# One attention and feed-forward kernel: a 16-bit shift in the weight decoding, softmax sums from the products, dummy transposes, and a second p buffer

## The chip, the cores and the metric

The kernel runs on one core of a Trainium2 chip. A core has five engines that follow their own instruction queues in order: PE (TensorE, products and transposes), DVE (VectorE), ACT (ScalarE), POOL (GpSimd) and SP (SyncE), which here issues all transfers. The metric is the device time of the core in microseconds, the median of several runs; lower is better.

## The reference

For 4 batches of 768 positions and 8 heads of 64, each position attends to its 31 neighbours and to 24 block summaries (the maximum of 32 keys, the mean of 32 values). The result, as x of 512 columns, goes through a layer norm and a two-layer network in double-precision weights, and is added to itself.

```python
k_sum = k.reshape(B, H, nb, block, D).max(axis=3)
v_sum = v.reshape(B, H, nb, block, D).mean(axis=3)
mask_l = np.abs(pos[:, None] - pos[None, :]) < window
scores_s = scale * np.einsum('bhsd,bhnd->bhsn', q, k_sum) + np.log(block)
scores_all = np.concatenate([np.where(mask_l, scores_l, -1e9), scores_s], axis=-1)
a = np.exp(scores_all - np.max(scores_all, axis=-1, keepdims=True))
a = a / (np.sum(a, axis=-1, keepdims=True) + 1e-09)
x = np.matmul(a, np.concatenate([v, v_sum], axis=2))      # then (B, S, 512)
xn = (x - mu) / np.sqrt(var + 1e-06) * g_ln
out = x + np.maximum(xn @ w_ch1, 0.0) @ w_ch2             # 512x2048, 2048x512, float64
```

## The kernel before, in words

The 3072 positions are 24 tiles T of 128. Attention works in 48 blocks t = 2T + hh: four heads of one tile. The keys that a block needs (158 neighbours' positions and 24 summaries) lie side by side in one operand of 184 to 192 columns, so that scores, softmax and the product with v each take one pass. The feed-forward part works in pairs of tiles, g = 0 to 11, in steps s = 8g + j: `g1` makes 256 of the 2048 hidden columns (tile h), `g2` multiplies them back into x (tile a). Each operand is split into two float16 halves, and three products of the halves stand for one in full precision. Relu writes hh (ACT) and the rest hl (DVE), and PE needs both.

Batch 0 (blocks 0 to 11, steps named `early_...` and `...0`) is done in float32 from whole tensors loaded at the start, since no scale for float16 is known yet: `fetch_k0`, `fetch_q` (qw), `fetch_v0` (vw), `fetch_tail` (vst: 32 more rows of v, and 24 rows of block means that `batch_v0` makes with PE and copies with ACT). A block does `early_k` (kx), `early_qk` (s), `softmax` (DVE subtracts the mask, scales and takes the minimum in one custom instruction into p and mn; ACT takes the exponential and, with `accum_out`, the row sums), `early_transp` (PE turns p, ACT copies it: pp to pT), `early_pv` (o; then rc = 1 / (sum + 1e-9) on DVE, and x = o times rc on DVE for t < 4, on ACT behind that). From block 12 on, transposes of p and of xn go over DMA, operands are float16 halves, POOL makes the lower half of p (`transp`, tile p from p), and every block uses the one buffer `prob[0]`, tag "p"; batch 0 alternates between "p" and "p2".

Beside batch 0, the weights are loaded (`fetch_w`, raw: 32 pieces of 128 x 512 doubles), decoded from double to single precision by integer operations on DVE (`dec_w`), squared on ACT for a scale per block of pieces (`scale_w`), and split into float16 halves (`conv_w`, wp). A piece is a pair of 32-bit words per weight, low word first; the decoded word stands 3 bits to the left of the high word's place, with the low word's top 3 bits at its end.

The order of each engine's queue is written at build time. `Plan` records every operation, estimates costs (`cost`), simulates the engines (`schedule`, with a clock for PE that needs 3200 columns in each 3.41 us), and in `improve` keeps the best of 32 simulated orders. `Plan.issue` (L333 to L349) writes the operations in order of their planned starts; all instructions therefore carry line L349 in the profile, and groups are told apart by their tiles. On the chip each queue runs in that order and waits where a tile is not ready. Buffers are tags: `work(tag, ...)` reuses the space of the tag's earlier tile when that one is dead; HOMES lists the tags that a kind of tile takes in turn. PSUM has four pools (s, o, h, a) of two buffers.

Of the kernel before, what the change touches and what calls it, by code (L numbers as in the profile page):

```python
# [15 lines left out]
F16 = mybir.dt.float16  # L16
U32 = mybir.dt.uint32
# [13 lines left out]
NE = 192  # L31
NG = TT // 2
# [8 lines left out]
EH = 4  # L41
# [13 lines left out]
AWAY = 24  # L55
LOADS = [("fetch_k0", 0), ("fetch_k0", 1), ("fetch_q", 0), ("gain",), ("fetch_blocks",), ("fetch_k0", 2), ("fetch_k0", 3)]
# [3 lines left out]
    ksg=("qke", "k0_0", "k0_1"),  # L60
# [35 lines left out]
class Plan:  # L96
# [11 lines left out]
    def __init__(self):  # L108
        self.ops, self.slots, self.prev, self.uses = [], {}, {}, {}
        self.joined = False  # L110
# [87 lines left out]
    def cost(self, engine, op, a, k, ins, outs):  # L198

        free = lambda x: math.prod(n for _, n in x.ap[1:])  # L200
        n = max(free(x) for x in ins + outs) if engine != "tensor" else free(a[0])
        if engine == "sync":
            x = (outs + ins)[0]
            return self.ISSUE.get(self.names[self.stage][0], 380), x.ap[0][1] * free(x) * mybir.dt.size(x.dtype) / (200.0 if "transpose" in op else 360.0)
        if engine == "tensor":
            dt = ins[-1].dtype
            if dt == F32R:
                return 0.443 * max(n, 256) + 4.5, 0.0
            if dt == F16 or op == "transpose":
                return max((1 if dt == F16 else 2) * n / 2.4 + 3.0, 28.0), 0.0  # L210
            return max(2 * n / 2.4 + 2.0, 100.0) * 2 if ins[0].ap[0][1] > D else 2 * n / 2.4 + 53.0, 0.0
        psum = any(x.space == bass.MemoryType.PSUM for x in ins)
        pointers = sum(1 for x in ins[1:] if free(x) == 1)
        if engine == "scalar":
            extra = ("accum_out" in k) + sum(isinstance(k.get(x), bass.AP) for x in ("scale", "bias"))
            weights = self.names[self.stage][0] in ("dec_w", "conv_w")
            return n / 1.2 + (51 if psum else 93) + 93 * extra + 35 * weights, 0.0
        if engine == "vector":
            fixed = {"tensor_tensor_reduce": 78, "reciprocal": 90}.get(op, 70) + 61 * pointers
            fixed += 119 * (self.box(ins[0])[1] == D)  # L220
# [28 lines left out]

    def slack(self, x, y):  # L250

        name, a = self.names[x.stage]
        if x.engine == "tensor":
            if name in ("g1", "g2"):
                return SLACK2 * (a[0] >= 24)
            return SLACK * (name in ("qk", "pv", "batch_s"))
        late = name in ("load_q", "load_k", "load_v", "softmax", "transp", "pv") and a[0] >= LATE
        late |= name[:5] == "batch" and a[0] >= 2
        late |= name in ("ln", "lnT") and a[0] >= LATE // 2
        late |= name in ("g1", "g2") and a[0] >= 24  # L260
        if not late:
            return 0.0
        return SLACKD if y.engine == "sync" else SLACKE

    def schedule(self, rank, after, back):
# [11 lines left out]
        port, half = 0.0, 0  # L277
# [3 lines left out]
        for _ in range(count):  # L281
# [17 lines left out]
            if e == "tensor" and not back:  # L299
                while t >= tick + self.TICK:  # L300
# [14 lines left out]
            for j, wait in before[i]:  # L315
                ready[j] = max(ready[j], free[e] if wait is None else end[i] + wait)
                left[j] -= 1
                if not left[j]:
                    heapq.heappush(coming[self.ops[j].engine], (ready[j], j))
        return start, end  # L320

    def improve(self, rank, after, then, rounds):

        best = None
        for _ in range(rounds):
            rank = [r if x.first is None else -1e9 + x.first for r, x in zip(rank, self.ops)]
            start, end = self.schedule(rank, after, False)
            if best is None or max(end) < best[0]:
                best = max(end), start, end
# [3 lines left out]
    def issue(self, nc):  # L333
        for x in self.ops:
            x.first = in_front(self.names[x.stage], x.engine)
        after = [self.waits(x) for x in self.ops]
# [9 lines left out]
        self.time, self.start, self.end = best  # L346
        for _, i in sorted(zip(best[1], range(len(after)))):
# [6 lines left out]
def body(ctx: ExitStack, tc, qt, qa, qe, kt, ks, va, vb, vs, g_ln, w1, w2, blocks, out):  # L354
# [18 lines left out]
    vst = [cp.tile([P, 2, 4, D], F32, name=f"vst{i}") for i in range(NV)]  # L373
# [10 lines left out]
    tails = [x.rearrange("p h j d -> p h (j d)") for x in vst]  # L384
# [6 lines left out]
    vw = [work(f"vw{T}", f"vw{T}", [P, DM])[:] for T in range(NT)]  # L391
# [23 lines left out]
    def clear():  # L415
# [83 lines left out]
    def batch_v0(c):  # L499
        if c == 0:  # L500
            bt["ps", 0] = psum("a", "v0", [P, DM])
        x = vw[c] if c < NT else vend
# [3 lines left out]
        if c == NT:  # L506
            for r in (32, 96):
                v = r // D
                for i in range(NV):
                    nc.scalar.copy(  # L510
                        tails[i][r : r + NB, :, v * P : v * P + P],
                        bt["ps", 0][r : r + NB, :].rearrange("p (h x) -> p h x", h=2)[:, :, v * P : v * P + P],
# [118 lines left out]
    def softmax(t, pr):  # L631
        T = t // 2
        var = 0 if T % NT == 0 else (2 if T % NT == NT - 1 else 1)
        if pr == 0:
            st[t, "p"] = prob[t < NEARLY and t % 2]
            st[t, "mn"] = work("mn", f"mn{t}", [P, 4], F32, 2)
            st[t, "sum"] = work("sum", f"sum{t}", [P, 4], F32, 2)
        p, mn, sm, ps = st[t, "p"], st[t, "mn"], st[t, "sum"], st[t, "s", pr]
        late_ = t >= NEARLY

        heads = [(2 * pr + u, 2 * pr + u, bt["mask", T // NT][:, var]) for u in range(2)] if late_ else [
            (2 * v + pr, 2 * pr + v, emask[:, var] if v else msk[:, var]) for v in range(2)
        ]
        for u, (j, i, mk) in enumerate(heads):
            w = mk.shape[1]
            nc.vector.tensor_tensor_reduce(
                p[:, i, :w], ps[:, u, :w], mk, -1.0 if late_ else -QSCALE, 3.0e38, ALU.add, ALU.min,
                mn[:, j : j + 1],
            )
        scale = -1.0  # L650
        if late_:
            m2, (scale, plus) = mn[:, 2 * pr : 2 * pr + 2], bt["c", T // NT]
            nc.gpsimd.tensor_scalar(m2, m2, plus, 0.0, ALU.mult, ALU.add)
        for j, i, mk in heads:
            x = p[:, i, : mk.shape[1]]
# [22 lines left out]
    def fetch_tail(T):  # L678

        for v in range(2):  # L680
            nc.sync.dma_start(
                tails[T % NV][v * D : v * D + BLK, :, v * P : v * P + P],
# [45 lines left out]
    def early_pv(t, pr):  # L728
        T, hh = divmod(t, 2)
        near = vw[T].rearrange("p (h j d) -> p h j d", h=2, j=4)[:, hh]  # L730
        tail = tails[T % NV].rearrange("p h (v u d) -> p h v u d", v=2, u=2)[:, hh, :, pr]
        if pr == 0:
            st[t, "o"] = psum("o" if t < 8 else "s", f"o{t}", [P, 8, D])
        ps, e = st[t, "o"][:, :4], st[t, "pt", pr]
        spare_cols = st[t, "o"][:, 4:6].rearrange("p a b -> p (a b)")
        with pl.unit():
            for _ in range(t < WARMV):
                nc.tensor.transpose(spare_cols, ident[:], ident[:])
            both = ps.rearrange("p (v u) d -> p v u d", v=2)[:, :, pr]
            nc.tensor.matmul(both, e[:, 1, :], tail, start=True, stop=False)  # L740
            for v in range(2):
                j = 2 * v + pr
                nc.tensor.matmul(ps[:, j, :], e[:, 2 * v, :], near[:, j], start=False, stop=v == 1)
# [3 lines left out]
        nc.vector.tensor_scalar(rc[:], st[t, "sum"][:], 1e-9, None, ALU.add)  # L747
# [4 lines left out]
        if t < PVS:  # L752
            nc.vector.tensor_tensor(xo, ps, rc.unsqueeze(2).to_broadcast([P, 4, D]), ALU.mult)
        else:
            for j in range(4):
                nc.scalar.activation(xo[:, j], ps[:, j], AF.Copy, scale=rc[:, j : j + 1])
# [72 lines left out]
    def dec_w(m):  # L829
# [130 lines left out]

    def attend(t):
# [18 lines left out]
        if t % 2 and t < 8:  # L980
            norm(t // 2)

# [126 lines left out]
```

## Time and profile before

| | |
|---|---|
| median of 3 runs | 637.73 us (633.65 to 638.5) |
| the profiled execution, its own time | 638.03 us |
| its span, first to last instruction | 636.2 us |
| PE, DVE, ACT, POOL busy | 610.9, 450.8, 391.5, 207.8 us |
| mean granted TensorE clock | 0.984 |

A group's row gives engine, operation, output and input tiles, shapes, count, busy time and mean nanoseconds of one, then the idle time of the engine in front of the group and who ended it. In a timeline a row begins with its start and length in us; a bracket is the idle time before it and the instruction that ended it. In the view by stretches a row has, after the stretch and its length, the busy time of PE, PEld, DVE, ACT and POOL with their instruction counts, the granted clock, the DMA share and GB/s. PE's matmuls are pipelined, so that the length of one is longer than the step to the next; the same holds in part for DVE and ACT, where the cost of an instruction in a full queue is the step from its start to the next start.

### The profile page before, as it was taken

What the parts mean: (1) busy time and instruction counts of PE and PEld (TensorE: products, weight loads), DVE (VectorE), ACT (ScalarE), POOL (GpSimd) and SP (SyncE); (2) the same over time, 40 slices, a digit from 0 to 9 for tenths busy, and PEclk for the clock granted to TensorE, in tenths of its full rate; (3) what the DMA queues carried; (4) which work ended last, traced back from release to release, by engine and by line L of the source; (5) the groups of instructions that cost most, each with busy time, mean ns of one, the idle gap of its engine ahead of it and who ended that gap; (6) DMA issues with size and microseconds to landing.
All of it is one profiled execution on the core that took longest, in us unless ns stands there. A gap on an engine that the chain in (4) does not pass through costs nothing.

```text
span 636.2 us, 13437 instructions
## 1 busy us (share of the span) xinstructions
PE 610.9 (96%) x4611; PEld 433.3 (68%) x4611; DVE 450.8 (71%) x1190; ACT 391.5 (62%) x1036; POOL 207.8 (33%) x412
## 2 busy tenths in 40 slices
PE   8957899999999899999979999999999999999997
PEld 6746776765776676776757677677677666666665
DVE  3899889999779998878989797657447734422212
ACT  3998798888888868778877577645446531110100
POOL 4221312024455545555555354333223321100000
PEclk9988799999999999999998999999999999999999
DMA  8980487526986977798778657465335412110000
GB/s 281 349 297 22 133 280 237 183 74 165 269 194 175 216 185 187 152 254 211 192 189 177 121 141 170 116 125 125 84 93 116 102 37 60 25 51 1 18 16 34
DMA packets 124997, 93.15 MB, mean 146 GB/s; under 512 B 84864, under 2 KB 107392, under 8 KB 124928
## 3 DMA queue, kind: packets, MB, share of 16 engines
q1 hardware_dynamic: 124928, 92.29, 55.7%
q8 instruction: 36, 0.59, 0.4%
q14 instruction: 33, 0.27, 0.1%
HBM read 66.27 MB, written 6.29 MB: 114 GB/s over the span
## 4 chain that ended last, share of the span: by engine, by line
PE 52%; DVE 25%; DMA 8%; ACT 6%; POOL 4%; issue 4%; SPq 1%; DVEq 0%; ACTq 0%; POOLq 0%
PE a L349 23%; PE h L349 23%; DVE x L349 3%; DVE p L349 3%; DMA ksg<-in_kt 3%; DVE wf L349 2%; ACT p L349 2%; PE o L349 2%; DVE hl L349 2%; PE s L349 2%; POOL p L349 2%; DVE qhl L349 2%; DVE kl L349 2%; DVE v L349 2%; DVE wp L349 1%
## 5 line engine op out<-in xcount | busy, mean ns | idle before, releaser
L349 PE MATMUL h<-xs,wp 128*128 128x256 f16 x2304 | 278.2, 276 | 6.7 <-DVE hl L349 4.8
L349 PEld LDWEIGHTS <-wp 128*128 128x128 f16 x2304 | 226.7, 99 | 53.6 <-DVE hl L349 5.2
L349 PE MATMUL a<-wp,hh 128*128 128x512 f16 (+1 forms) x768 | 226.5, 377 | 0.3 <-DVE x L349 0.3
L349 PE MATMUL a<-wp,hl 128*128 128x512 f16 x384 | 144.7, 377 | 0.2 <-DVE hl L349 0.2
L349 ACT ACTIVATE hh<-h 128x512 f16<-128x512 f32 x96 | 56.6, 589 | 123.3 <-PE h L349 99.3
L349 DVE SCALAR_TENSOR_TENSOR hl<-h,hh 128x512 f16<-128x512 f32 x96 | 65.7, 685 | 86.8 <-ACT hh L349 86.6
L349 PEld LDWEIGHTS <-hh 128*128 128x128 f16 x784 | 75.3, 98 | 61.7 <-issue 0.9
L349 ACT ACTIVATE p<-p,mn,sv 128x184 f32<-128x184 f32 x144 | 76.0, 530 | 24.3 <-POOL mn L349 20.9
L349 POOL TENSOR_TENSOR p<-p,p 128x512 f16<-128x512 f32 x72 | 72.3, 1010 | 35.0 <-ACT p L349 33.2
L349 PEld LDWEIGHTS <-hl 128*128 128x128 f16 x392 | 38.3, 98 | 45.4 <-DVE hl L349 1.1
L349 DVE CUSTOM_DVE_ANT_0 p<-s,mask 128x184 f32<-128x184 f32 x144 | 42.2, 343 | 16.6 <-POOL p L349 10.0
L349 POOL TENSOR_SCALAR mn<-mn,sv 128x2 f32<-128x2 f32 x72 | 32.4, 451 | 58.3 <-DVE mn L349 57.3
L349 POOL TENSOR_TENSOR x<-x,rc 128x256 f32<-128x256 f32 x36 | 25.5, 709 | 75.5 <-DVE x L349 75.4
L349 DVE SCALAR_TENSOR_TENSOR x<-a,wsc,x 128x512 f32<-128x512 f32 (+1 forms) x48 | 35.5, 739 | 19.6 <-PE a L349 19.2
L349 ACT ACTIVATE kh<-ksg,sv 128x368 f16<-128x368 f32 x72 | 42.7, 595 | 10.0 <-POOL ksg L349 9.9
L349 DVE SCALAR_TENSOR_TENSOR kl<-ksg,sv,kh 128x368 f16<-128x368 f32 x72 | 44.5, 643 | 3.3 <-PE s L349 3.2
L349 DVE SCALAR_TENSOR_TENSOR v<-vst,sv,v 128x256 f16<-128x256 f32 x72 | 40.4, 588 | 2.3 <-ACT v L349 2.0
L349 POOL COPY ksg<-ksum 128x48 f32<-128x48 f32 x72 | 24.3, 338 | 47.9 <-DMA ksg<-in_kt 44.5
L349 DVE TENSOR_REDUCE x<-o 128x256 f32<-128x512 f32 x36 | 24.6, 685 | 16.2 <-PE o L349 15.9
L349 ACT CAST p<-p 128x512 f16<-128x512 f32 x72 | 33.1, 509 | 0.3
L349 ACT ACTIVATE v<-vst,sv 128x512 f16<-128x512 f32 x36 | 25.6, 716 | 8.8 <-PE o L349 7.2
L349 PEld LDWEIGHTS <-qhl 128*128 128x128 f16 x288 | 24.4, 99 | 5.2 <-issue 0.3
(124 smaller groups left out, 786.0 us busy)
## 6 DMA issues: line engine op xcount, KB each, us to landing
raw<-in_w SPq DMA_DIRECT2D x32, 512.0 KB
ksg<-in_kt SPq DMA_DIRECT2D x72, 184.0 KB
out_x<-x SPq DMA_DIRECT2D x23, 256.0 KB
qw<-in_qt SPq DMA_DIRECT2D x36, 128.0 KB
vst<-in_va SPq DMA_DIRECT2D x36, 128.0 KB
qs<-in_qt SPq DMA_DIRECT2D x36, 128.0 KB
vst<-in_vb SPq DMA_DIRECT2D x84, 32.0 KB
bst<-in_ks SPq DMA_DIRECT2D x12, 192.0 KB
```

What stands on the lines that cost most here:

```text
L349: getattr(getattr(nc, self.ops[i].engine), op)(*a, **k)
```

## The change

Decoding (`dec_w`): the low halves of the high words are overwritten in place with the low words' top 16 bits shifted right by 13, a tensor_scalar over 16-bit elements; one scalar_tensor_tensor then puts the sign, the top exponent bit and these three bits together with the shifted word. Before it was a tensor_scalar and two scalar_tensor_tensors.

Batch 0's softmax: the exponentials no longer write sums. vw and the vst tiles get a column of ones beside each pair of heads (130 columns for 128), so the products give the sums in o, and rc is made from them. The v loads become two transfers per tile; memsets write the ones. In the order of heads, mn and p now agree.

Dummy transposes: a step `spare`, recorded after block 3, is one transpose of the identity into pool "a". The simulation notes every pause of PE over 800 ns between its place and the first operation that needs its PSUM slot, and `issue` writes further copies of that transpose into these pauses, up to 800 ns before the next planned operation.

Late p: blocks from 12 on alternate between "p" and a new tile p3 in the tag "k0_0". The key buffers ksg go from ("qke", "k0_0", "k0_1") to ("qke", "k0_1", "qw4"), and the mask emask moves into "qke". EH = 6 puts the transposes of blocks 4 and 5 into pool "h" as well.

```diff
-EH = 4
+EH = 6
+NV2 = 2 * D + 2
+FILL_IN, FILL_END = 500, 800
-    ksg=("qke", "k0_0", "k0_1"),
+    ksg=("qke", "k0_1", "qw4"),
...
+    def watch(self):
+        spare = [i for i, x in enumerate(self.ops) if self.names[x.stage][0] == "spare"]
+        self.opens = spare[0] if spare else None
+        self.closes = {i for i, x in enumerate(self.ops) if self.opens in x.after}
...
+                if i == self.opens:
+                    opened = t
+                closed |= i in self.closes
+                at = max(free[e], opened or t)
+                while not closed and t - at > FILL_IN and t - at > FILL_END:
...
+                    fills.append(at)
+                    at += 112 if warm else 224
+                    columns += 256
...
-        for _, i in sorted(zip(best[1], range(len(after)))):
+        for _, i in sorted([*zip(best[1], range(len(after))), *((t, -1) for t in fills)]):
+            if i < 0:
+                op, a, k = self.ops[self.opens].calls[0]
+                getattr(nc.tensor, op)(*a, **k)
+                continue
...
-    emask = work("emask", "emask", [P, 3, NE])[:]
+    emask = work("qke", "emask", [P, 3, NE])[:]
...
+        for x in vw:
+            nc.vector.memset(x[:, :, :: NV2 - 1], 1.0)
...
-        for x in vst:
+        for x in tails:
             nc.gpsimd.memset(x[:], 0.0)
+            for v in range(2):
+                nc.gpsimd.memset(x[v * D : v * D + BLK + NB, :, v, :: NV2 - 1], 1.0)
...
     def go_late():
-        nc.gpsimd.memset(prob[0][:, :, NC:], 0.0)
+        late["p"] = prob[0], work("k0_0", "p3", [P, 4, NE])
+        for x in late["p"]:
+            nc.gpsimd.memset(x[:, :, NC:], 0.0)
...
-            nc.sync.dma_start(vw[c].rearrange("p (h x) -> p h x", h=2), va[c].rearrange("h k j d -> k h (j d)"))
+            for h in range(2):
+                nc.sync.dma_start(
+                    vw[c][:, 2 * h : 2 * h + 2, 1 : NV2 - 1], va[c, h].rearrange("k (v u) d -> k v (u d)", v=2)
+                )
...
-            st[t, "p"] = prob[t < NEARLY and t % 2]
+            st[t, "p"] = (prob if t < NEARLY else late["p"])[t % 2]
...
+            for j, mk in heads:
+                x = p[:, j, : mk.shape[1]]
+                nc.scalar.activation(x, x, AF.Exp, bias=mn[:, j : j + 1], scale=-1.0)
+            return
...
-            both = ps.rearrange("p (v u) d -> p v u d", v=2)[:, :, pr]
-            nc.tensor.matmul(both, e[:, 1, :], tail, start=True, stop=False)
+            nc.tensor.matmul(ps[:, :, cols], e[:, 1, :], tail, start=True, stop=False)
...
-        nc.vector.tensor_scalar(rc[:], st[t, "sum"][:], 1e-9, None, ALU.add)
+        nc.vector.tensor_scalar(
+            rc.rearrange("p (v u) -> p v u", v=2), ps[:, :, :: NV2 - 1], 1e-9, None, ALU.add
+        )
...
-        nc.vector.scalar_tensor_tensor(x[:], hw, 0xC0000000, x[:], ALU.bitwise_and, ALU.bitwise_or)
+        halves = raw[m].bitcast(U16).rearrange("p x (t h) -> p x t h", t=2)
+        low, top = halves[:, :, 1, 0], halves[:, :, 0, 1]
+        nc.vector.tensor_scalar(low, top, 13, None, ALU.logical_shift_right)
...
-        nc.vector.scalar_tensor_tensor(y, lw, 29, x[:], ALU.logical_shift_right, ALU.bitwise_or)
+        nc.vector.scalar_tensor_tensor(y, hw, 0xC0000007, x[:], ALU.bitwise_and, ALU.bitwise_or)
...
+    @pl.step
+    def spare():
+        ps = psum("a", "spare", [P, P])
+        nc.tensor.transpose(ps[:], ident[:], ident[:])
...
+        if t == 3:
+            spare()
```

More of the change, by code (lines that the diff above doesn't have):

```diff
@@ L16 @@
 F16 = mybir.dt.float16
+U16 = mybir.dt.uint16
 U32 = mybir.dt.uint32
@@ L276, in schedule @@
         ring, warm, columns, tick = 0.0 if back else self.FIRST, False, 0.0, 0.0
-        port, half = 0.0, 0
+        port, half, fills, opened, closed = 0.0, 0, [], None, False
         for i in range(count):
@@ L299, in schedule @@
             if e == "tensor" and not back:
+                if i == self.opens:
[3 more added lines that the diff above has]
+                while not closed and t - at > FILL_IN and t - at > FILL_END:
+                    while at >= tick + self.TICK:
+                        warm, columns, tick = columns >= 3200, 0.0, tick + self.TICK
+                    fills.append(at)
+                    at += 112 if warm else 224
+                    columns += 256
                 while t >= tick + self.TICK:
@@ L319, in schedule @@
                     heapq.heappush(coming[self.ops[j].engine], (ready[j], j))
+        if not back:
+            self.fills = fills
         return start, end
@@ L328, in improve @@
             if best is None or max(end) < best[0]:
-                best = max(end), start, end
+                best = max(end), start, end, self.fills
             rank = [-x for x in self.schedule([-x for x in end], then, True)[1]]
@@ L345, in issue @@
         best = self.improve(rank, after, then, ROUNDS)
-        self.time, self.start, self.end = best
-        for _, i in sorted(zip(best[1], range(len(after)))):
+        self.time, self.start, self.end, fills = best
+        for _, i in sorted([*zip(best[1], range(len(after))), *((t, -1) for t in fills)]):
[3 more added lines that the diff above has]
+                continue
             for op, a, k in self.ops[i].calls:
@@ L372, in body @@
     ident = cp.tile([P, P], F32, name="ident")
-    vst = [cp.tile([P, 2, 4, D], F32, name=f"vst{i}") for i in range(NV)]
+    tails = [cp.tile([P, 2, 2, NV2], F32, name=f"vst{i}") for i in range(NV)]
+    vst = [x.rearrange("p h v x -> p (h v x)")[:, : 8 * D].rearrange("p (i j d) -> p i j d", i=2, j=4) for x in tails]
     ones = cp.tile([P, P], F32, name="ones")
@@ L390, in body @@
     qw = [work(f"qw{T}", f"qw{T}", [P, DM])[:] for T in range(NT)]
-    vw = [work(f"vw{T}", f"vw{T}", [P, DM])[:] for T in range(NT)]
+    vw = [work(f"vw{T}", f"vw{T}", [P, 4, NV2])[:] for T in range(NT)]
     vend = work("bst", "vend", [BLK, DM])[:]
     kx = [work(f"kx{x}", f"kx{x}", [P, 2, NE])[:] for x in range(2)]
-    emask = work("emask", "emask", [P, 3, NE])[:]
+    emask = work("qke", "emask", [P, 3, NE])[:]
     @pl.step
@@ L501, in batch_v0 @@
             bt["ps", 0] = psum("a", "v0", [P, DM])
-        x = vw[c] if c < NT else vend
+        x = vw[c][:, :, 1 : NV2 - 1] if c < NT else vend
         n = x.shape[0]
@@ L634, in softmax @@
         if pr == 0:
-            st[t, "p"] = prob[t < NEARLY and t % 2]
+            st[t, "p"] = (prob if t < NEARLY else late["p"])[t % 2]
             st[t, "mn"] = work("mn", f"mn{t}", [P, 4], F32, 2)
[L637 to L643, printed above, removed]
@@ L644, in softmax @@
-        for u, (j, i, mk) in enumerate(heads):
-            w = mk.shape[1]
+            if t >= NEARLY:
+                st[t, "sum"] = work("sum", f"sum{t}", [P, 4], F32, 2)
+        p, mn, sm, ps = st[t, "p"], st[t, "mn"], st.get((t, "sum")), st[t, "s", pr]
+        if t < NEARLY:
+            heads = [(2 * pr + v, emask[:, var] if v else msk[:, var]) for v in range(2)]
+            for v, (j, mk) in enumerate(heads):
+                w = mk.shape[1]
+                nc.vector.tensor_tensor_reduce(
+                    p[:, j, :w], ps[:, v, :w], mk, -QSCALE, 3.0e38, ALU.add, ALU.min, mn[:, j : j + 1]
+                )
[3 more added lines that the diff above has]
+            return
@@ L646, in softmax @@
+        mk = bt["mask", T // NT][:, var]
+        for u in range(2):
+            j = 2 * pr + u
             nc.vector.tensor_tensor_reduce(
-                p[:, i, :w], ps[:, u, :w], mk, -1.0 if late_ else -QSCALE, 3.0e38, ALU.add, ALU.min,
-                mn[:, j : j + 1],
-            )
[L650 to L655, printed above, removed]
+                p[:, j, :NC], ps[:, u], mk, -1.0, 3.0e38, ALU.add, ALU.min, mn[:, j : j + 1]
+            )
@@ L656, in softmax @@
+        m2, (scale, plus) = mn[:, 2 * pr : 2 * pr + 2], bt["c", T // NT]
+        nc.gpsimd.tensor_scalar(m2, m2, plus, 0.0, ALU.mult, ALU.add)
+        for u in range(2):
+            j = 2 * pr + u
+            x = p[:, j, :NC]
             nc.scalar.activation(x, x, AF.Exp, bias=mn[:, j : j + 1], scale=scale, accum_out=sm[:, j : j + 1])
```

38 lines of the change are left out of this document (22 added, 16 removed).

## The prediction

> **What bounds the kernel now.** The page comes first: how long, and which engine is busy.
>
> ```profile
> span 636.2 us, 13437 instructions
> ...
> PE 610.9 (96%) x4611; PEld 433.3 (68%) x4611; DVE 450.8 (71%) x1190; ACT 391.5 (62%) x1036; POOL 207.8 (33%) x412
> ```
>
> PE is the bound by its share, with 25.3 us idle (636.2 - 610.9). An average hides where. The view by stretches, next, has busy time of PE, PEld, DVE, ACT and POOL (instructions in brackets), then granted clock, DMA share, GB/s.
>
> ```profile
> 25.00:65.00 40.00, 29.11 (x207) 24.04 (x205) 39.29 (x121) 36.84 (x119) 7.89 (x20) 0.86 0.58 205
> 65.00:80.00 15.00, 13.33 (x94) 10.71 (x94) 13.36 (x35) 10.66 (x30) 5.29 (x10) 0.79 0.38 119
> 80.00:131.00 51.00, 50.27 (x382) 36.92 (x380) 47.26 (x124) 44.99 (x133) 6.66 (x16) 1.00 0.69 218
> 131.00:320.00 189.00, 186.89 (x1469) 130.31 (x1468) 166.78 (x440) 152.57 (x399) 97.08 (x166) 1.00 0.79 194
> 320.00:340.00 20.00, 16.40 (x132) 11.91 (x131) 17.73 (x57) 15.76 (x40) 11.93 (x21) 0.91 0.74 177
> 340.00:600.00 260.00, 260.00 (x1987) 181.56 (x1986) 146.84 (x365) 114.07 (x271) 69.19 (x127) 1.00 0.40 92
> ```
>
> Three regimes. From 25 to 65 us DVE is full (39.3 of 40) and ACT nearly (36.8), while PE idles 10.9 us and runs at a mean clock of 0.86: here the decoding of the weights sets the pace. From 80 us on PE is full, except for 3.6 us lost around 330. After 340 nothing but PE matters. So the end moves by what PE gets done sooner before 80 us, and by the hole at 330; work saved on DVE or ACT after 131 us is worth nothing. The half-clock time, by the same view:
>
> ```profile
> 45.50:50.70 5.20, 5.19 (x25) 3.68 (x26) 5.20 (x11) 2.19 (x6) 0.00 (x0) 0.50 0.06 18
> 61.00:67.80 6.80, 5.92 (x27) 4.84 (x28) 6.55 (x15) 6.57 (x24) 0.00 (x0) 0.50 0.56 180
> 74.60:78.00 3.40, 3.40 (x18) 2.34 (x17) 3.22 (x11) 2.36 (x7) 0.92 (x1) 0.50 0.41 116
> 334.00:337.40 3.40, 2.98 (x15) 2.23 (x16) 3.32 (x9) 3.40 (x10) 2.14 (x3) 0.51 0.64 177
> ```
>
> The sum is made against the profiled execution, 638.0 us (span 636.2); the median of the runs, 637.7, lies 0.3 below it.
>
> **The 16-bit shift.** One decode is three DVE instructions; the timeline of DVE shows them, and the view of the raw weights' tile counts them between 25 and 80 us.
>
> ```profile
> 45.95 0.42 DVE L349 TENSOR_SCALAR wf<-raw 128x512 uint32<-128x512 uint32 x1
> 46.28 0.69 DVE L349 SCALAR_TENSOR_TENSOR raw<-raw,wf 128x512 uint32<-128x512 uint32 x1
> 46.88 0.68 DVE L349 SCALAR_TENSOR_TENSOR wf<-raw,wf 128x512 uint32<-128x512 uint32 x1
> ...
> L349 DVE SCALAR_TENSOR_TENSOR raw<-raw,wf x17: 665/686/701, 25.5 to 76.2; 128x512 uint32<-128x512 uint32 x17
> L349 DVE TENSOR_SCALAR wf<-raw x15: 410/420/445, 29.3 to 72.3; 128x512 uint32<-128x512 uint32 x15
> L349 DVE SCALAR_TENSOR_TENSOR wf<-raw,wf x15: 659/682/689, 30.1 to 74.9; 128x512 uint32<-128x512 uint32 x15
> ```
>
> From start to start a tensor_scalar holds DVE 0.33 us (45.95 to 46.28) and a scalar_tensor_tensor 0.60 (46.28 to 46.88). The change turns one of the two 0.60s into a tensor_scalar over the same 512 elements of two bytes, at the same step of 8 bytes. No row shows two-byte integers at a step. Bounds: 0.33, the one-source form, and 0.60, the two-source form. I take 0.33: the tensor_scalar of the rows already reads at that step, and the write at that step (raw, 686 ns) costs what the dense one does (wf, 682), so neither side shows a charge for the step. That is 0.27 a decode: 15 decodes, 4.0 us, on an engine that is the bound there. The 14 decodes after 80 us would save 3.8, but PE idles only 0.7 (51.00 - 50.27) in their stretch: I take 0.5. Bounds of the edit: 0 and 7.8.
>
> [...]
>
> **Sums from products.** Each batch-0 exponential loses the read of its accumulator.
>
> ```profile
> 11.13 0.19 ACT L349 ACTIVATION_READ_ACCUMULATOR p<-p,mn 128x1 f32 x1
> 11.22 0.43 ACT L349 ACTIVATE p<-p,mn 128x184 f32<-128x184 f32 x1
> ...
> L349 ACT ACTIVATION_READ_ACCUMULATOR p<-p,mn 128x1 f32 x48 | 9.2, 191 | 0.0
> 37.91 0.17 DVE L349 TENSOR_SCALAR rc<-sum 128x4 f32<-128x4 f32 x1 [0.18 <-ACT p L349]
> 38.65 0.17 DVE L349 RECIPROCAL rc<-rc 128x4 f32<-128x4 f32 x1
> 39.15 0.49 PE L349 MATMUL o<-vst,pT 128*128 128x128 f32 x2
> 45.51 1.09 PE L349 MATMUL tx<-ident,xn 128*128 128x128 f32 x4 [5.48 <-DVE xn L349]
> ```
>
> The read takes 0.09 of ACT's time (11.13 to 11.22): 48 make 4.3 us. ACT is the second engine of that stage, so this lets DVE's 4.0 through and adds nothing; without it the cover would be gone, since ACT has only 3.2 idle in 25 to 65. Against it: rc and its reciprocal now stand behind the products (at 37.91 and 38.65 they came before those of 39.15), two instructions of 0.17 ahead of x, and DVE's queue behind them waits too. x feeds xn, for which PE waited 5.48. I charge 0.3; bounds 0 and 12 blocks x 0.34 = 4.1. One more column per 64 in the products is 1.6% of the o rows: nothing.
>
> The v loads become 12 instead of 6, with pieces of half the size; SP issues them in order, ahead of the raw weights.
>
> ```profile
> 4.08 4.11 SPq L349 DMA_DIRECT2D vw<-in_va  x6
> 8.36 0.34 SPq L349 DMA_DIRECT2D vend<-in_vb  x1
> 22.40 0.43 DVE L349 TENSOR_SCALAR wf<-raw 128x512 uint32<-128x512 uint32 x1 [1.41 <-DMA raw<-in_w]
> 3.81 0.95 DVE L349 TENSOR_REDUCE kmax<-k 128x24 f32<-128x768 f32 x1 [3.81 <-DMA k<-in_ks]
> 6.75 0.20 POOL L349 COPY kx<-kmax 128x24 f32<-128x24 f32 x1
> ```
>
> Six issues at 0.34 are 2.0 us, at their present spacing (4.11/6) 4.1; the bytes stay, and 1.41 of DVE's wait at 22.40 shows that raw weights are just late there. I charge 0.8; bounds 0 and 4.1. The memsets of ones go into DVE's idle 3.81 us and beside POOL's start-up, whose key copy ends at 6.95 while the warm-up transposes run to 8.1 (below): nothing, and some tenths if POOL is later than that. The new homes of the mask, of the key buffers and the h slots for blocks 4 and 5 move waits of batch 0's end, under a full PE: nothing; if that cover fails, a load's wait, as in the last rival.
>
> **Dummy transposes.** They fill PE's planned pauses over 0.8 us between the first norm's transposition and the first g2. Can a transpose hold the clock up? Windows of the warm-up's own tile (PE, PEld), then two pauses from PE's timeline:
>
> ```profile
> 1.70:6.30 4.60, 4.60 (x22) 4.60 (x23) 1.00 0.84 246
> 6.40:8.10 1.70, 1.70 (x16) 1.46 (x14) 1.00 0.97 349
> 61.75 0.90 PE L349 MATMUL pp<-ident,p 128*128 128x128 f32 x3 [2.37 <-ACT p L349]
> 73.89 0.28 PE L349 MATMUL h<-xs,wp 128*128 128x256 f16 x1 [1.35 <-DVE hl L349]
> ```
>
> 22 transposes took 4.60 us (0.209 each), the next 16 took 1.70 (0.106). Nothing but transposes had run on PE, so they raised its rate to the full one (the clock column's 1.00 in the first row is no event: the rate shows half). [...]
>
> Half clock before 80 us covers 5.19 + 5.92 + 3.40 = 14.5 us of PE work, worth 7.3. The first two lie under a full DVE, which pays for nothing; the third leads straight into PE's full stretch: 1.7 us gained. Bounds: 7.3 gained, and a loss of the dummies themselves where the work behind them is ready early: (5.48 - 0.8) + (2.37 - 0.8) + (1.35 - 0.8) = 6.8 us.
>
> **Second late p buffer.** The hole at 330, in the timelines of DVE, POOL and PE:
>
> ```profile
> 328.02 2.21 POOL L349 TENSOR_TENSOR p<-p,p 128x512 f16<-128x512 f32 x1
> 328.11 1.10 DVE L349 SCALAR_TENSOR_TENSOR kl<-ksg,sv,kh 128x368 f16<-128x368 f32 x2
> 331.29 0.35 DVE L349 CUSTOM_DVE_ANT_0 p<-s,mask 128x184 f32<-128x184 f32 x1 [2.08 <-POOL p L349]
> 333.69 0.68 DVE L349 SCALAR_TENSOR_TENSOR hl<-h,hh 128x512 f16<-128x512 f32 x1
> 328.20 2.78 PE L349 MATMUL h<-xs,wp 128*128 128x256 f16 x24
> 334.42 2.74 PE L349 MATMUL h<-xs,wp 128*128 128x256 f16 x12 [3.44 <-DVE hl L349]
> ```
>
> The softmax of the next block waits 2.08 us until POOL has read the only late p; hl stands behind it on DVE, and PE waits 3.44 for hl, then works 3.4 us at half clock (1.7 lost). With two buffers the 2.08 goes. [...] Gain 2.1 + 1.7 = 3.8; bounds 0 (another wait in that place) and 5.1.
>
> **Sum.** 638.0 - 4.0 - 0.5 - 1.7 - 3.8 + 0.3 + 0.8 = 629.1; less the 0.3 to the median, 629.
>
> **Rivals.**
> [...] Chance 0.17, with 0.05 of it for a cost between the two. [...]
> (b) The hole at 330 stays, as POOL itself is late (2.21 for that subtraction) and hl waits for another of its products: 629 + 3.8 = 632.8. Chance 0.13.
> [...] Chance 0.04.
> (d) More comes through: all 7.8 of the shift, 7.3 of the clock and 5.1 at the hole: 638.0 - 20.2 = 617.8, less 0.3: 617.5. For it speaks that PE idles 12.6 us between 25 and 80; against it, that DVE stays full. Chance 0.08.
> (e) Slower. All orders are written anew, and softmax no longer held by p runs ahead on DVE. At each of the three batch switches (330 is one; the others pass unharmed today) an instruction that waits for a late load then stands before hl, and PE pays as at 334: 3.4 + 1.7 = 5.1. From the second such stall the change is within 1%, with three 629 + 15.3 = 644.3. For it: the plan that left the hole at 330 did not foresee it. Against it: 340 to 600 has none in 260 us. Chance 0.07.
>
> **How the numbers follow.** The forecast has 0.51, its own range 623 to 633 (each term within half of itself). A measurement of this kernel tells about 1% from no change: below 631.4 counts as faster, above 644.1 as slower. Faster: 0.43 of the forecast, (c) 0.03, (d) 0.08, some of (a) and (b) 0.07: 0.61. Slower: most of (e) with a little from dummies in the way: 0.07. Same: 0.32. The range 618 to 640 leaves out (e), half of (d) and the ends of unknown costs, under 0.2 together.
>
> **What would show it.** [...] The 48 accumulator reads gone, the rc rows after o. Half-clock time before 80 us well under the 15.4 us of the three rows above, with extra transposes in the pauses. No DVE p waiting 2 us on POOL p, no half clock near 330. PE full from before 77 us instead of 80. Wrong would be: 25 to 65 us with DVE full and PE no further, PE's queue with dummies while the work behind is ready, or a new wait of hl.

## The result and the profile after

The kernel after takes 632.95 us (median of 13 runs, 632.21 to 634.79), the kernel before beside it 637.41 (13 runs, 633.65 to 638.83): a ratio of 0.9931, 95% interval 0.9914 to 0.9949. The change gains 4.5 us, 0.7%, where the forecast had 8.7 (637.7 to 629). The time lies in the forecast's range of 618 to 640, and nearest to what the prediction wrote for rival (b) alone (632.8), and to 633.5, the forecast with no gain from the shift (629 + 4.5).

The page of after, its own time 634.28 us: span, busy time by engine, and two lines of the slices (PE's busy tenths and the granted clock, some 16 us a slice).

```profile
span 632.5 us, 13475 instructions
...
PE 611.5 (97%) x4661; PEld 433.9 (69%) x4661; DVE 447.1 (71%) x1196; ACT 388.0 (61%) x988; POOL 206.3 (33%) x419
...
PE   7988899899999999999999999999999999999997
...
PEclk8999999999999999999999999999999999999999
```

PE's busy time is where it was (610.9 before), but it now holds 50 transposes of the identity, 49 of them the added copies; its idle time went from 25.3 to 21.0 us, and DVE and ACT were relieved by 3.7 and 3.5 us. Now the view by stretches of after, its columns as before, then the only stretch at half clock, one that before did not have, and the transposes of the identity:

```profile
25.00:65.00 40.00, 34.68 (x280) 29.21 (x279) 38.70 (x127) 36.67 (x100) 9.74 (x23) 1.00 0.61 220
65.00:80.00 15.00, 14.06 (x125) 11.93 (x125) 14.90 (x42) 11.97 (x36) 3.74 (x10) 1.00 0.49 140
80.00:131.00 51.00, 47.56 (x350) 34.45 (x348) 49.02 (x127) 44.57 (x120) 10.41 (x17) 1.00 0.70 224
131.00:320.00 189.00, 186.44 (x1493) 133.07 (x1492) 165.43 (x434) 151.79 (x397) 91.47 (x168) 1.00 0.77 190
320.00:340.00 20.00, 20.00 (x146) 13.76 (x145) 15.59 (x43) 13.20 (x35) 7.08 (x14) 1.00 0.68 157
...
12.10:15.50 3.40, 3.40 (x6) 1.43 (x5) 0.41 (x4) 1.04 (x3) 0.00 (x0) 0.50 0.74 207
...
L372 PE MATMUL spare<-ident x49: 272/273/307, 43.5 to 73.1; 128*128 128x128 f32 x49
```

From 25 to 80 us the clock is full throughout, and before's four stretches at half clock are gone. The hole at 330 is closed. What is new is the third row: from 80 to 131 us PE, which was full there (50.27), now idles 3.4 us, while DVE is busy 49.02 of 51. That DVE still sets the pace in this stage is a reading of the shares here; the experiments take it up.

The decode in after, in the view of DVE's groups between 80 and 131 us:

```profile
L375 DVE TENSOR_SCALAR raw<-raw 128x512 uint16<-128x512 uint16 x15 | 11.0, 747 | 0.0
...
L375 DVE TENSOR_SCALAR wf<-raw 128x512 uint32<-128x512 uint32 x14 | 6.0, 431 | 0.3 <-DMA raw<-in_w 0.3
```

And a shift with its follower on DVE's timeline, which gives start and length:

```profile
39.22 0.75 DVE L375 TENSOR_SCALAR raw<-raw 128x512 uint16<-128x512 uint16 x1
39.74 0.68 DVE L375 BATCH_NORM_STATS2 s<-x 128x6 f32<-128x512 f32 x1
```

747 ns, against 431 for the tensor_scalar over words. From start to start it holds DVE 0.52 us (39.22 to 39.74), where the step it replaces held it 0.60: 0.08 a decode, not 0.27. The start of batch 0 moved too. The timelines of SP's issues and of DVE's first decode, after, and the first decode of before:

```profile
4.08 9.71 SPq L375 DMA_DIRECT2D vw<-in_va  x12
13.84 0.60 SPq L375 DMA_DIRECT2D vend<-in_vb  x1
...
22.07 0.43 DVE L375 TENSOR_SCALAR wf<-raw 128x512 uint32<-128x512 uint32 x1 [3.91 <-DMA raw<-in_w]
...
16.84 0.42 DVE L349 TENSOR_SCALAR wf<-raw 128x512 uint32<-128x512 uint32 x1
```

The twelve v loads hold SP 9.71 us instead of 4.11, and the first decode starts at 22.07, where before it started at 16.84. This start differs from execution to execution: with the same loads in the same order, the profiled runs with narrowed shifts and without the dummies (both below) have 8.11 and 8.56 us of SP, and first decodes at 20.0 and 20.4.

### The profile page after: what moved, and what is told of

Its sections match the earlier page's. It is cut to its first block, busy times and chain, and to the rows that moved or that the text cites. A ratio compares the mean times of both kernels' runs of the same rounds, so it can differ in the third digit from the quotient of the medians.

```text
span 632.5 us, 13475 instructions
## 1 busy us (share of the span) xinstructions
PE 611.5 (97%) x4661; PEld 433.9 (69%) x4661; DVE 447.1 (71%) x1196; ACT 388.0 (61%) x988; POOL 206.3 (33%) x419
## 4 chain that ended last, share of the span: by engine, by line
PE 57%; DVE 17%; DMA 13%; ACT 8%; issue 3%; POOL 2%; SPq 1%; ACTq 0%; DVEq 0%; POOLq 0%
PE a L375 27%; PE h L375 24%; DMA raw<-in_w 4%; DMA ksg<-in_kt 3%; DVE raw L375 2%; ACT p L375 2%; DVE p L375 2%; PE s L375 2%; PE o L375 2%; DVE hl L375 2%; DVE kl L375 2%; DMA bst<-in_vs 2%; DVE qhl L375 1%; DVE x L375 1%; DVE vsum L375 1%
## 5 line engine op out<-in xcount | busy, mean ns | idle before, releaser
L375 PE MATMUL h<-xs,wp 128*128 128x256 f16 x2304 | 273.1, 273 | 0.8 <-DVE hl L375 0.5
L375 PEld LDWEIGHTS <-wp 128*128 128x128 f16 x2304 | 223.7, 98 | 42.7 <-DVE hl L375 1.5
L375 POOL TENSOR_TENSOR p<-p,p 128x512 f16<-128x512 f32 x72 | 69.6, 974 | 33.5 <-ACT p L375 31.5
L375 POOL COPY ksg<-ksum 128x48 f32<-128x48 f32 x72 | 22.6, 316 | 66.1 <-DMA ksg<-in_kt 62.0
L375 PEld LDWEIGHTS <-pT 128*128 128x128 f16 x432 | 23.7, 98 | 5.3 <-DMA pT<-p 1.3
```

The lines of the kernel that those rows point to most:

```text
L375: getattr(getattr(nc, self.ops[i].engine), op)(*a, **k)
```

## The experiments

Two kinds. Some kernels let the planner write a new order; others have the order of before or of after written in as a list, so that no engine's queue changes but for the edit ("fixed order"). Ratios are to the kernel before, run on the same chip in the same comparison, with the 95% interval. A ratio differs a little from the quotient of the two medians, so that the text says of a difference in us which of them it comes from.

**The second late p buffer alone, planned anew** (to the kernel before):

```diff
-    ksg=("qke", "k0_0", "k0_1"),
+    ksg=("qke", "k0_1", "qw4"),
-        nc.gpsimd.memset(prob[0][:, :, NC:], 0.0)
+        late["p"] = prob[0], work("k0_0", "p3", [P, 4, NE])
+        for x in late["p"]:
+            nc.gpsimd.memset(x[:, :, NC:], 0.0)
-            st[t, "p"] = prob[t < NEARLY and t % 2]
+            st[t, "p"] = (prob if t < NEARLY else late["p"])[t % 2]
```

> The kernel before with the second late p buffer alone (p3 in the tag k0_0, ksg in qke, k0_1, qw4). Theory 1, the gain is the hole at 330 us: PE's wait of 3.4 us and the half clock behind it go, 632 to 634 us against 637.4, ratio 0.991 to 0.995. Rival, the hole went only because all orders were written anew, and the gain came from the first 130 us: 636 to 639 us here, with DVE's softmax still not the one that PE waits for.

646.93 us, ratio 1.0167 (1.0119 to 1.0216): slower, which no theory had. Three rows of its view by stretches:

```profile
65.00:80.00 15.00, 10.43 (x67) 8.51 (x68) 13.19 (x30) 10.72 (x33) 3.52 (x8) 0.78 0.39 129
...
131.00:320.00 189.00, 180.62 (x1432) 129.31 (x1430) 161.29 (x436) 149.00 (x397) 85.70 (x156) 0.99 0.77 185
320.00:340.00 20.00, 20.00 (x161) 14.15 (x159) 17.02 (x46) 14.50 (x36) 9.42 (x16) 1.00 0.79 163
```

The hole at 330 is closed, and yet PE has lost 2.9 us in 65 to 80 and 6.3 in 131 to 320 against before. The order that came with the buffer lost far more than the buffer could win: 9.1 us by the medians. So a part's price can't be read from a kernel that is planned anew; the runs named with before's or after's own order keep it fixed.

**The same buffer in before's own order.** The edit is the same, except that ksg's list is here ("qke", "qw3", "k0_1"), and

```diff
-        best = self.improve(rank, after, then, ROUNDS)
+        seq = [...]      # the order that the planner gave the kernel before
```

> The kernel before with its own order of every engine's instructions written in as a list, and only the second late p buffer added (one more memset of 64 small columns on POOL in batch 0; the k staging tiles change homes). Nothing else is planned anew. Theory (the buffer is what opens the hole): DVE no longer waits for POOL's casts of p between 320 and 340 us, PE's busy time there goes from 16.40 to 19 or more, and the time falls by 3.0 to 5.5 us, a ratio of 0.991 to 0.995. Rival (the hole belongs to the order and only the new order of the kernel after closed it): PE stays below 18 in that window and the ratio is 0.998 to 1.002. A third outcome, the hole gone and the time not shorter, would say that PE catches the loss up later.

633.27 us, ratio 0.9947 (0.9921 to 0.9972). The time fell as the theory said, but not at its place. The view by stretches of this kernel:

```profile
65.00:80.00 15.00, 13.72 (x114) 11.34 (x114) 13.87 (x35) 10.93 (x33) 5.69 (x13) 0.92 0.37 114
...
131.00:320.00 189.00, 187.73 (x1475) 130.36 (x1474) 169.10 (x448) 153.29 (x401) 93.70 (x167) 1.00 0.81 196
320.00:340.00 20.00, 16.74 (x139) 12.52 (x137) 17.69 (x50) 16.15 (x44) 11.05 (x21) 0.91 0.75 176
```

And its waits of PE and of DVE between 320 and 340 us (total, times, longest):

```profile
PE h L427 <- DVE hl L427: 2.9, 1, 2.9
...
DVE xn L427 <- POOL rs L427: 1.6, 1, 1.6
```

No softmax waits for POOL's p any more. But the hole stays: PE 16.74 instead of 16.40, and of its wait for hl 2.9 us are left of 3.4, because DVE, let on, now stands 1.6 us before xn until POOL delivers rs, with hl behind xn in its queue. That is the case "another wait in that place". The half clock behind that wait stays too: 0.91 in 320 to 340, as in before. Of the 3.8 us between the two spans, 1.2 lie after 131 us (0.84 in 131 to 320 and 0.34 in 320 to 340). About 2 lie in 65 to 80, where the granted clock was 0.92 instead of 0.79; late p is used from block 12 on, and before that block the buffer adds a memset on POOL and no more. The runs say the same: the mean granted clock is 0.9861 over those of this kernel and 0.9842 over those of before, and the difference, of 636 us, is about 1.2 us (an estimate). How much of the 3.4 us (by the ratio) belongs to the buffer is therefore not settled; 1.2 is what the trace shows at places that it reaches.

**One late p buffer in the kernel after**, planned anew: `late["p"] = prob[0], prob[0]`.

> The changed kernel with one late p buffer as before. Theory 1: softmax waits on POOL's subtraction again (some 10 us of DVE waits in all), and the time goes back to 636 to 639 us. Rival, the order did it: 632 to 634 us, as the changed kernel.

635.69 us, 0.998 (0.9953 to 1.0007): 2.7 us above after by the medians. Seven waits for POOL's p are back on DVE between 131 and 600 us (7.4 us in all). Yet the hole isn't there with one buffer either:

```profile
131.00:320.00 189.00, 185.54 (x1471) 129.99 (x1469) 168.68 (x450) 154.96 (x408) 95.56 (x167) 1.00 0.79 196
320.00:340.00 20.00, 20.00 (x167) 14.64 (x166) 19.62 (x53) 17.15 (x46) 11.21 (x19) 1.00 0.77 186
```

**A new order by itself.** The kernel before, with one number of the planner changed:

```diff
-SLACKD, SLACKE, LATE = 1000, 150, 14
+SLACKD, SLACKE, LATE = 1000, 160, 14
```

> The kernel before with the same instructions, in an order planned anew after one of the planner's waits was set from 150 to 160 ns: the work is the same, only the order differs. It measures what a new order is worth by itself. Theory (order is a small term): ratio 0.997 to 1.003. Rival (order is as large as the parts of the change, as the 647 us of the run with a second buffer and a new order would have it): off by more than 0.005 to either side.

637.59 us, 1.002 (0.9999 to 1.0041). Its rows of the same view:

```profile
80.00:131.00 51.00, 48.09 (x355) 34.52 (x354) 46.64 (x123) 43.41 (x130) 5.92 (x14) 1.00 0.65 215
131.00:320.00 189.00, 185.64 (x1465) 129.55 (x1464) 168.78 (x439) 151.08 (x396) 91.69 (x167) 1.00 0.80 192
320.00:340.00 20.00, 20.00 (x172) 15.19 (x171) 19.77 (x58) 16.74 (x42) 11.88 (x19) 1.00 0.76 191
```

With the same instructions and one late p, the hole at 330 is gone (PE 3.6 us better there), and PE has lost 2.2 us in 80 to 131 and 1.25 in 131 to 320 instead: the time is the same. So the hole comes and goes with the order. A new one moves such losses about, here for nothing, with the second buffer for 9 us more.

**The shift alone, in before's own order:**

```diff
-        nc.vector.scalar_tensor_tensor(x[:], hw, 0xC0000000, x[:], ALU.bitwise_and, ALU.bitwise_or)
+        nc.vector.tensor_scalar(low, top, 13, None, ALU.logical_shift_right)
-        nc.vector.scalar_tensor_tensor(y, lw, 29, x[:], ALU.logical_shift_right, ALU.bitwise_or)
+        nc.vector.scalar_tensor_tensor(y, hw, 0xC0000007, x[:], ALU.bitwise_and, ALU.bitwise_or)
```

> The kernel before in its own order, with the decode's second step replaced by the 16-bit shift in place and nothing else. By the prediction's price (0.27 us a decode, 15 decodes before 80 us and half a microsecond for the later ones) the time falls by 4.5 us, ratio 0.993. By what the trace of after shows (749 ns a shift against 686 for the step it replaces, next instruction 0.52 us after its start) each decode gains under 0.1 us: 1 to 2 us in all, ratio 0.997 to 0.999. Rival (PE's own order sets the time, DVE's gain stays unused): 1.000 and no change of PE's busy time in 25 to 80 us.

635.52 us, 0.9993 (0.9966 to 1.002): 0.4 us by the ratio, 1.3 by the medians (before's runs beside it: 636.8), and by the interval at most 2.2, where the prediction had 4.5. The runs can't tell a gain of 1 us from none.

**What makes the shift slow.** After, with the shift of a piece written to or read from a dense scratch tile, by the piece's number:

```diff
-        nc.vector.tensor_scalar(low, top, 13, None, ALU.logical_shift_right)
+        if m % 4 == 0:
+            nc.vector.tensor_scalar(h16[:], top, 13, None, ALU.logical_shift_right)
+        elif m % 4 == 1:
+            nc.vector.tensor_scalar(low, h16[:], 13, None, ALU.logical_shift_right)
+        elif m % 4 == 2:
+            nc.vector.tensor_scalar(h16[:], h16[:], 13, None, ALU.logical_shift_right)
+        else:
+            nc.vector.tensor_scalar(low, top, 13, None, ALU.logical_shift_right)
```

> Measures the shift by itself: after, with the shift of one weight piece in four written densely into a scratch tile, of one in four read densely from it, of one in four both, and the rest as they are, so the low three bits of three weight pieces in four are wrong. Stepped means every fourth 16-bit element for the read, every second 32-bit word's low half for the write. [...] Rival (16-bit integer operands cost by themselves): all four forms take about 749 ns. If only one side costs, one of the two half-dense forms is as slow as the in-place one and the other as fast as the dense one.

Its groups of DVE (h is here the scratch tile; the mean of the first row contains one instruction of 1.58 us):

```profile
L375 DVE TENSOR_SCALAR raw<-raw 128x512 uint16<-128x512 uint16 x8 | 6.8, 851 | 0.0
L375 DVE TENSOR_SCALAR raw<-h 128x512 uint16<-128x512 uint16 x8 | 5.9, 738 | 0.0
L375 DVE TENSOR_SCALAR h<-raw 128x512 uint16<-128x512 uint16 x8 | 3.3, 415 | 4.5 <-DMA raw<-in_w 4.5
L375 DVE TENSOR_SCALAR h<-h 128x512 uint16<-128x512 uint16 x8 | 2.3, 286 | 0.0
```

DVE's timeline gives for each form the step to the next start: dense, stepped read, stepped write, both.

```profile
41.79 0.28 DVE L375 TENSOR_SCALAR h<-h 128x512 uint16<-128x512 uint16 x1
41.99 0.69 DVE L375 BATCH_NORM_STATS2 s<-x 128x6 f32<-128x512 f32 x1
...
28.75 0.41 DVE L375 TENSOR_SCALAR h<-raw 128x512 uint16<-128x512 uint16 x1
29.08 0.17 DVE L375 RECIPROCAL rc<-rc 128x4 f32<-128x4 f32 x1
...
36.97 0.74 DVE L375 TENSOR_SCALAR raw<-h 128x512 uint16<-128x512 uint16 x1
37.50 0.66 DVE L375 BATCH_NORM_STATS2 s<-x 128x6 f32<-128x512 f32 x1
...
63.96 0.74 DVE L375 TENSOR_SCALAR raw<-raw 128x512 uint16<-128x512 uint16 x1
64.48 0.67 DVE L375 BATCH_NORM_STATS2 s<-x 128x6 f32<-128x512 f32 x1
```

Dense on both sides an instruction takes 286 ns and holds DVE 0.20 us; with a stepped read alone 415 and 0.33; with a stepped write alone 738 and 0.53, as much as with both (0.52). So two-byte elements are not slow by themselves, which rules the rival out, and the step of the write sets the price here; the stepped read costs far less. A single run took 627.62 us.

**DVE relieved of the shift, in after's own order**, each shift narrowed to one column:

```diff
-        nc.vector.tensor_scalar(low, top, 13, None, ALU.logical_shift_right)
+        nc.vector.tensor_scalar(low[:, :1], top[:, :1], 13, None, ALU.logical_shift_right)
```

> The kernel after in its own order, with each of the 32 shifts narrowed from 512 columns to one: the low three bits of all other weights are not put in, which is left out of the computation here. DVE is relieved of about 0.45 us in each of 32 decodes, 14 us, all before 140 us. Theory (DVE sets the pace up to 131 us: it is busy 49.02 of the 51 us from 80 on): PE's idle time up to 131 us shrinks from 10 us to 4 or less and the time falls by 5 to 8 us below after, to a ratio of 0.980 to 0.985 to before. Rival (PE's order and the arrival of the weights set it, DVE's load is beside the point): within 1.5 us of after, ratio 0.991 to 0.995.

626.75 us, 0.9842 (0.9809 to 0.9875). Its stretches:

```profile
25.00:65.00 40.00, 36.16 (x300) 31.36 (x300) 37.64 (x138) 38.04 (x107) 7.89 (x21) 1.00 0.64 229
65.00:80.00 15.00, 13.85 (x125) 11.87 (x124) 13.10 (x41) 12.31 (x34) 4.05 (x13) 1.00 0.50 156
80.00:131.00 51.00, 49.57 (x357) 35.02 (x356) 46.30 (x137) 45.98 (x125) 8.77 (x20) 1.00 0.64 211
```

With no queue's order changed, the relief of DVE alone takes some 6 us off (6.2 below after by the medians, 5.7 by the ratios): PE gains 1.5 in 25 to 65 and 2.0 in 80 to 131, where it had lost 2.7 in after. PE's idle time from 25 to 131 us falls from 9.7 to 6.4, not to the 4 of the theory. DVE's work up to 131 us sets the end. A narrowed shift still holds DVE some 0.11 us, so about 13 us (32 x 0.41) of its work went, and the end moves by 0.44 to 0.47 us for each. These two profiles lie 9.5 us apart, more than the medians: 1.4 us of PE's gain fall before 25 us, where hardly a shift has run, and 1.9 between 131 and 320.

**The dummies not written**, after's own order otherwise: `*((t, -1) for t in fills[:0])`.

> The changed kernel in the very same order, without the copies of the dummy transpose. If they hold the clock up and that reaches the end: half clock returns between 43 and 78 us, 634 to 636 us. If the stage is DVE's and PE's rate there pays for nothing: half clock returns, but 632.5 to 633.5 us. If transposes do not count for the clock: the same half-clock stretches with and without them, which the profile of the changed kernel already speaks against.

635.06 us, 0.9974 (0.9949 to 0.9999): above after by 2.1 us by the medians and 2.7 by the ratios, whose intervals just meet. Half clock is back, in two stretches above all:

```profile
44.10:50.90 6.80, 4.42 (x22) 3.32 (x24) 6.36 (x13) 3.80 (x9) 1.53 (x2) 0.50 0.37 81
61.10:67.90 6.80, 5.39 (x25) 4.54 (x26) 6.51 (x14) 5.92 (x19) 0.00 (x0) 0.50 0.45 123
```

**Six v loads in the kernel after**, from an extra copy of v that the host lays out in that form, planned anew:

```diff
-            for h in range(2):
-                nc.sync.dma_start(vw[c][:, 2 * h : 2 * h + 2, 1 : NV2 - 1], ...)
+            nc.sync.dma_start(vw[c][:, :, 1 : NV2 - 1], vn[c])
```

> The changed kernel with six loads of v into the rows with ones, from an input that holds the same values by tile, row and pair of heads. If the twelve loads are what brought the first decode from 16.8 to 22.1 us: the first raw weights are asked for before 14 us instead of 17.8, the first decode starts by 19 us, and 1 to 4 us of it reach the end: 629 to 632 us. Rival, DVE has enough other work and the start is paid for nothing: first decode earlier, 632 to 634 us. If the time of the loads is the number of pieces and not of transfers: first decode still at 21 to 22 us.

632.7 us, 0.9948 (0.9919 to 0.9978): as after. SP's timeline at the loads and DVE's at the first decode:

```profile
4.07 6.74 SPq L375 DMA_DIRECT2D vw<-in_vn  x6
...
17.81 0.43 DVE L375 TENSOR_SCALAR wf<-raw 128x512 uint32<-128x512 uint32 x1
```

And a stretch in which PE loses more than after does:

```profile
80.00:131.00 51.00, 45.95 (x332) 32.91 (x330) 45.94 (x121) 41.64 (x113) 8.45 (x17) 1.00 0.63 208
```

The decoding starts 4.3 us sooner, and PE idles 5.0 us in 80 to 131 instead of 3.4, with DVE idle as much (45.94 of 51). DVE's amount of work alone doesn't account for that; the order is a new one, and PE's longest wait in the stretch is 1.7 us, for ACT's squares. So the price of the loads can't be read from this run.

**All but the products with ones**: before with the shift, the dummies and the second buffer, the code of each as in after, with the old sums and v tiles, planned anew.

> The change without the products with ones: the kernel before with the 16-bit shift, the dummy transposes and the second late p buffer, but with the accumulator reads of batch 0's sums, its old v tiles and its six v loads. Planned anew. Theory (the parts add, and the products with their twelve loads bring nothing): the parts measured apart, 3.4 us for the buffer, 0.5 for the shift and 2.1 for the transposes, take 6 us off, ratio 0.989 to 0.992, at or below after; the first decode starts near 17 us as before. Rival (the products carry part of the gain, through the 48 accumulator reads that ACT loses and DVE's earlier p): ratio 0.996 to 1.000, with ACT's busy share in 25 to 80 us above that of after.

634.57 us, 0.9955 (0.9929 to 0.9982). That is between the theories and overlaps with after (0.9914 to 0.9949). The parts measured apart would make 6 us; together they make 2.9 by the ratio. But this kernel has an order of its own, so that the parts don't add is not shown by it, nor what the products with their loads are worth: the two ratios differ by 1.5 us, with either sign inside their intervals.

**The planner told the shift's true length**, after otherwise:

```diff
-            return n / (1.92 if op == "tensor_scalar" and not psum else 0.96) + fixed, 0.0
+            fast = 1.14 if ins and ins[0].dtype == U16 else 1.92
+            return n / (fast if op == "tensor_scalar" and not psum else 0.96) + fixed, 0.0
```

> The kernel after, with one number of its planner changed: the cost that it puts down for the 16-bit shift of 512 columns goes from 0.34 us to 0.52 us, which is the time from a shift's start to the next instruction's in the trace of after. Same instructions, new order. Theory (DVE sets the pace up to 131 us and the order is made for a DVE that is faster than it is): PE's idle time between 65 and 131 us falls below the 4.4 us of after and the time by 1 to 3 us, ratio 0.988 to 0.992. Rival (DVE's work is what counts, in whatever order): within 1.5 us of after, ratio 0.991 to 0.996.

633.4 us, 0.9934 (0.9908 to 0.9959): the rival's outcome. PE's idle time in 65 to 131 did fall a little, from 4.4 to 4.1 us, but a better informed order brings no time back.

**No shift at all**, two steps a decode, planned anew:

```diff
-        nc.vector.tensor_scalar(low, top, 13, None, ALU.logical_shift_right)
```

> The kernel after without the shift: two steps a decode, DVE relieved of 32 steps of 0.52 us, 16.6 us in all before 140 us, planned anew. The low three of the 24 bits of every weight are then not those of the input but the lowest three of its own upper word, an error of up to seven units of the last place, which is left out of the computation here. Theory (DVE sets the pace up to 131 us, whatever the order): at or below the run with narrowed shifts in after's order, 622 to 627 us, ratio 0.977 to 0.985. Rival (what that run gained came from its order meeting an emptier DVE, and a new order gives it back): 628 to 633 us, ratio 0.986 to 0.993.

625.84 us, 0.9821 (0.9782 to 0.9861), faster than before and after. The stretch in question:

```profile
80.00:131.00 51.00, 50.14 (x369) 36.29 (x368) 42.48 (x115) 44.22 (x122) 7.46 (x17) 1.00 0.64 213
```

PE is full there again with DVE at 42.48. It is no drop-in for after: the weights carry three bits fewer. It shows what a decode would gain that got these bits at no cost to DVE: 7.1 us against after, by the medians.

## Why the prediction was right and wrong

**What bounds the kernel: right, and too narrow.** That DVE's work in the weight stage sets the end is shown by the run with narrowed shifts in after's order (some 6 us below after); the one without shifts, in a new order, agrees (7.1). The prediction let that stage end at 80 us, since PE was full from there in before. In after it reaches on to 131, and "PE full from before 77 us" did not come: 47.56 of 51.

**The shift: the step that failed.** "I take 0.33", because "neither side shows a charge for the step", was read from rows over four-byte words, and the row for the write was of a two-source instruction, which holds DVE 0.60 us with a dense write too; what a stepped write costs the faster one-source form, no row showed. For two-byte elements the trace has 0.52 from start to start, and the write's step is what costs. Alone in before's order the edit was worth 0.4 us by the ratio and 1.3 by the medians, instead of 4.5. Worked out, 0.08 x 29 decodes are 2.3 us of DVE's work, and at the 0.44 to 0.47 us per us that the narrowed shifts gave, about 1 us. The prediction gave a cost between its two bounds, 0.33 and 0.60, a chance of 0.05. In the run that measures the shift by itself, the stepped read alone held DVE 0.33 us, no longer than the tensor_scalar over words at the same step (0.33), and the words' rows show no charge for the write (686 against 682 ns). No row had the right element size and step together, and half of the forecast's gain hung on the choice.

**The dummies: right.** They hold the clock (before had three half-clock stretches between 44 and 80 us, after's order without them two of 6.8 us, and after has none there: its one of 3.4 us, from 12.1 us on, lies ahead of the dummies), and leaving them out costs 2.1 us by the medians (2.7 by the ratios), against the 1.7 of the sum. That transposes do not count for the clock, the last outcome named before the run without the copies, is out.

**The second buffer: the wait went, the hole's cause was named wrongly.** DVE's waits between 131 and 600 us had in before the row

```profile
DVE p L349 <- POOL p L349: 10.0, 8, 2.2
```

and in after, as in before's order with two buffers, no wait of p for POOL's p is left. So "with two buffers the 2.08 goes" held. That PE's wait falls by as much, to 1.36 us (3.44 - 2.08), failed: in before's order 2.9 us stay, behind POOL's rs, which on POOL stands behind the subtractions of p; this is what rival (b) described. The 1.7 for the clock took for granted that such a rest leaves the clock up. No run shows that term: in before, half clock from 74.6 us follows a wait of 1.35; in before's order with two buffers the granted clock from 320 to 340 us stayed at 0.91 behind the wait of 2.9; and in before's order with the shift alone it was 1.00 there, with a wait of 3.1 us for hl. The hole is closed in after as it is in the two kernels with a single late p that were planned anew. The term of 3.8 stands beside 3.4 in before's order, of which about 1.2 is seen where the buffer acts, and 2.7 in a new order; its size was near, its mechanism was not shown, and where the rest comes from is open.

**The loads: more than was charged at the start, the price at the end is open.** 0.8 was charged, with 4.1 as the upper bound; in the profile of after the decoding started 5.2 us later, in two others with the same order 3.2 and 3.5. With six loads and a new order the time was that of after, with the lead lost again before 131 us; in a fixed order this was not run. The 48 accumulator reads are gone and rc stands behind o, as described; of the 0.3 charged for that, PE shows one wait of 1.2 us for rc between 25 and 80 us. What the products are worth by themselves was not told apart.

**The sum.** The shift was put 3.2 to 4.1 us too high (4.5 against 1.3 or 0.4), which is most of the 4.2 us between forecast (8.7) and result (4.5). That the rest then comes out so near is partly chance: the second buffer's term was right in size without its mechanism, the loads came later than charged, and each new order brings gains and losses of several us of its own. Rival (e), a slower kernel through a rewritten order, did not come true here, but the run with the buffer alone (1.0167) shows that its kind exists: it had its losses in 65 to 80 and 131 to 320 us, not in three stalls at the batch switches.

## What to carry to other kernels

Here a duration did not carry over from one form of the instruction, element size and step of each side to another: the same shift took 286, 415 or 738 ns by its steps alone, while over words a stepped and a dense write lay 4 ns apart (686 and 682). Where the row for the new form is missing, keep the whole span open, and don't trust rows that come from another size. Work saved on the engine that sets the pace counts up to the point where another engine is full in the kernel *after*, so look for that point again. Where a planner rewrites the order, price a part with the order held fixed; the second buffer was worth -3.4 us in before's order and +9 planned anew.

## What the runs showed of the hardware

A tensor_scalar over 512 two-byte elements took 286 ns dense, 415 with a stepped read and 738 with a stepped write (0.20, 0.33 and 0.53 us to the next start). One over four-byte words with a stepped read took 422, and in a scalar_tensor_tensor over words a stepped write cost nothing (686 against 682). Six v loads held SP's queue 4.11 us in before and 6.74 when they wrote into the rows with ones; twelve of half the size into these rows held it 8.11 to 9.71 in three profiles of after's order. And the granted clock differs from run to run of one kernel: in the comparison with the fixed orders 28 runs of the kernel before had 0.975 to 0.989, and times of 632.9 to 639.1 us, the shorter ones mostly at the higher clocks; after had 0.991 to 1.000 and 632.2 to 634.8. Without the dummies, in after's order, the clocks were 0.980 to 0.992, so the dummies raise the clock. That they also narrow the spread of the times is not shown: the kernel with shift, dummies and second buffer had clocks of 0.991 to 0.997 and times of 629.7 to 637.4 us.
